# Chunked attention and a one-of-eight expert layer on one core: weights cast by the DMA, records scattered by expert, dense layers in token order

## The chip, the core and the metric

The kernel runs on one core of a Trainium2 chip. Five engines work from queues of their own and meet at semaphores: TensorE (PE; its weight loads are shown as PEld), VectorE (DVE), ScalarE (ACT), GpSimd (POOL) and SyncE (SP), which here only issues transfers. Sixteen DMA engines move the data; SP and POOL each have a queue to them. The metric is the device time of one execution in microseconds, lower is better.

## The reference: what is computed

Inputs are q, k, v (4 batches, 8 heads, 768 positions, 64 wide), eight memory keys and values per head, a gate and eleven weight matrices' worth of layers (two dense, eight experts of two).

```
for each chunk c of 32 positions:                  # attention
    k_full = [mem_k (8), k[c_start-16 : c_end+8]]   # v_full likewise
    a = softmax(q_c @ k_full.T / 8)
    out_c = a @ v_full
x = out as [3072 tokens, 512]                      # the expert layer
y_dense = relu(x @ w1_dense) @ w2_dense
e = argmax(x @ w_gate);  gate = softmax(x @ w_gate)[e]
y = y_dense + gate * (relu(x @ w1[e]) @ w2[e])
```

All weight matrices are 512x512 and lie in DRAM as f32: 18 of them, 1 MB each.

## The kernel before

**Attention.** The work goes in 16 pairs of heads (four pairs make one batch of 768 tokens, six tiles of 128). Each turn of the loop at L478 mixes two or three pairs: POOL casts q and k of pair i+1 to bf16 (`cast_qk`, L234), DVE scales pair i-1 (`scaled`), PE transposes q and k of i+1 (L249), turns back the probabilities of i (L306), transposes x of i-1 for the gate in f32 (`gate_part`, L356), makes scores (L268, L282), gate sums (L371) and values (L318). `load_qk` and `load_v` bring in pair i+2 on SP; `load_v` writes into one of three buffers `vw` that ACT first fills with the memory rows (L207). The order on every engine is the order in which the code is written.

**Weights.** One weight matrix per turn is loaded as f32 into one of three buffers `tmp` on SP (L91, behind the q, k and v loads of the turn) and cast to bf16 by POOL at the end of the next turn (L464). Thirteen are done so; the last five are cast by ACT after the attention.

**Routing.** When the four pairs of a batch are done, `choose` takes each token's expert and `rank` its place among the tokens of that expert. POOL writes the batch's records (x in bf16 and the gate, 1028 bytes) to `x_rec` in DRAM in token order (L449, one DMA). After the last batch DVE and PE turn the ranks into lists (`lane_p`, `lane_t`, `in_tile`; L523 to L581): for each of 31 slots of 128 tokens which expert it holds, which token rows to fetch and where to put the results.

**Slots.** The second stage (L659) takes 31 slots, each of one expert, padded. A slot's records are fetched by an indirect DMA from POOL four slots ahead (L604); PE transposes them (L613); DVE copies the expert's first layer to a fixed place (L635); PE then computes for the slot's tokens both the dense layers (L644 with `w1d`, L668) and the expert's (L644 with `w_st`, L681); DVE adds the two (L687) and POOL scatters the result rows to `out` (L690).

Of the kernel before, what the change touches and what calls it, by code (L numbers as in the profile page):

```python
# [20 lines left out]
def kernel(  # L21
# [31 lines left out]
    NW = 3  # L53
# [21 lines left out]
    wtmp_pool = ctx.enter_context(tc.tile_pool(name="wtmp", bufs=NW))  # L75
# [30 lines left out]
    lane = iota_f32(128, "lane")  # L106
    slot_no = iota_f32(NS, "slot_no")
    desc = iota_f32(E, "desc", base=E, step=-1)
    pcol = iota_f32(1, "pcol", step=0, cm=1)
    ones = r_pool.tile([128, 128], BF16, name="ones")  # L110
# [10 lines left out]
    onehot = r_pool.tile([128, NT, E], BF16, name="onehot")  # L121
    seen = r_pool.tile([128, E], F32, name="seen")
    nc.vector.memset(seen, 0.0)
    seen_bf = r_pool.tile([128, E], BF16, name="seen_bf")
    hi_f = r_pool.tile([128, NT], F32, name="hi_f")
    lane_p = r_pool.tile([128, NT, 128], BF16, name="lane_p")
    lane_t = r_pool.tile([128, NT, 128], BF16, name="lane_t")
    REC = D_moe // 2 + 1
    x_rec = tc.dram_tile([N_tokens, REC], F32, name="x_rec")


    with (
# [207 lines left out]
        def gate_part(pi):  # L340
# [3 lines left out]
            if hp == 0:  # L344
                lg_b = x_pool.tile([128, T, E], F32, tag="lg")
                rec_b = x_pool.tile([128, T, REC], F32, tag="rec")
                bat[b]["lg"], bat[b]["rec"] = lg_b, rec_b
            lg, rec = bat[b]["lg"], bat[b]["rec"]
            nc.gpsimd.tensor_copy(
                rec.bitcast(BF16)[:, :, hp * 128:(hp + 1) * 128], xb  # L350
            )
            xTs_ = []
            for t0 in (0, T // 2):
# [9 lines left out]
                xTs_.append(xT32)  # L363
            st_[pi]["xT"] = xTs_
# [15 lines left out]
        def choose(b):  # L380
# [11 lines left out]
            oh = onehot[:, b * T:(b + 1) * T, :]  # L392
# [8 lines left out]
            nc.vector.reciprocal(rec[:, :, REC - 1:REC], sm)  # L401
            bat[b]["here"] = here

        def rank(b):

            oh = onehot[:, b * T:(b + 1) * T, :]
            rk_ps = g_ps[:, 64:64 + T * E].rearrange("p (t e) -> p t e", e=E)
            nc.tensor.matmul(rk_ps, upper, oh, start=True, stop=False)
            for t in range(T - 1):
                nc.tensor.matmul(  # L410
                    rk_ps[:, t + 1:, :], ones,
                    oh[:, t:t + 1, :].to_broadcast([128, T - 1 - t, E]),
                    start=False, stop=(b == 0 and t == T - 2),
                )
            if b:
                nc.tensor.matmul(
                    rk_ps, ones, seen_bf[:, None, :].to_broadcast([128, T, E]),
                    start=False, stop=True,
                )
# [3 lines left out]
            nc.vector.reduce_sum(rk, val, axis=AX.X)  # L423
            nc.vector.tensor_tensor(seen, seen, bat[b]["here"][:, :, 0], ALU.add)
            nc.vector.tensor_copy(seen_bf, seen)
            rk_i = r_work.tile([128, T], I32, tag="rk_i")
            nc.vector.tensor_copy(rk_i, rk)
            hl_i = r_work.tile([128, 2, T], I32, tag="hl_i")
            nc.vector.tensor_scalar(hl_i[:, 0], rk_i, 127, None, ALU.bitwise_and)
            nc.vector.tensor_scalar(hl_i[:, 1], rk_i, 7, None, ALU.logical_shift_right)  # L430
            lo = r_work.tile([128, T], F32, tag="lo")
            nc.vector.tensor_copy(lo, hl_i[:, 0])
            nc.vector.tensor_copy(hi_f[:, b * T:(b + 1) * T], hl_i[:, 1])
            bat[b]["lo"] = lo

        def lanes(b):
            lo = bat[b]["lo"]
            for t in range(T):
                n = b * T + t
                nc.vector.tensor_scalar(  # L440
                    lane_p[:, n, :], lane, lo[:, t:t + 1], pcol, ALU.is_equal, ALU.mult
                )
                nc.vector.tensor_scalar(
                    lane_t[:, n, :], lane, lo[:, t:t + 1], float(n + 1),
                    ALU.is_equal, ALU.mult,
                )

        def rows_out(b):
            nc.gpsimd.dma_start(  # L449
                x_rec[b * S:(b + 1) * S, :].rearrange("(t p) c -> p t c", p=128),  # L450
                bat[b]["rec"],
            )

        w_todo = list(range(len(w_list)))
        w_tmp = []
        LATE = 5

        def weight_load():
            i = w_todo.pop(0)
            w_tmp.append((i, load_w(*w_list[i])))  # L460

        def weight_cast(eng):
            i, tmp = w_tmp.pop(0)
            eng(w_list[i][1], tmp)  # L464

        with tc.manual_schedule(engines={PE_, DVE_, ACT_, POOL_, SP_}):
            load_qk(0)
            load_small()
            load_qk(1)
            for i in range(2):  # L470
                mem_rows(i)
                load_v(i)
            mem_keys()
            cast_qk(0)
            transpose_qk(0)
            scores(0)
            softmax(0)
            for i in range(NPAIR):  # L478
                nxt = i + 1 < NPAIR
                b, hp = divmod(i, NP)  # L480
                if nxt:
                    cast_qk(i + 1)
                if i + 2 < NPAIR:
                    load_qk(i + 2)
                if i:
                    scaled(i - 1)
                if nxt:
# [236 lines left out]
```

## Time and profile before

| | before |
|---|---|
| median of 3 runs (lowest to highest) | 356.83 us (353.12 to 362.11) |
| the profiled execution | 355.28 us |
| its span, first to last instruction | 353.6 us |
| attention, to the end of the last values | 0 to 202.0 us |
| lists and first fetch | 202.0 to 226.7 us |
| slots | 226.7 to 345.1 us |
| busy: PE, DVE, ACT, POOL | 262.1, 156.1, 141.8, 145.4 us |

Read it in this order. The page gives busy time per engine and, in 40 slices, where it lies, with the clock that PE was granted and how busy the DMA engines were. The windows view gives the same for chosen stretches, with the bytes per second. The timeline gives single instructions: start, length, engine, line, operation, and in brackets the idle time before it and what ended that. A matmul row's length includes the pipeline, so the distance between starts tells what a block of matmuls takes.

### The profile page before, as it was taken

What the parts mean: (1) busy time and instruction counts of PE and PEld (TensorE: products, weight loads), DVE (VectorE), ACT (ScalarE), POOL (GpSimd) and SP (SyncE); (2) the same over time, 40 slices, a digit from 0 to 9 for tenths busy, and PEclk for the clock granted to TensorE, in tenths of its full rate; (3) what the DMA queues carried; (4) which work ended last, traced back from release to release, by engine and by line L of the source; (5) the groups of instructions that cost most, each with busy time, mean ns of one, the idle gap of its engine ahead of it and who ended that gap; (6) DMA issues with size and microseconds to landing.
All of it is one profiled execution on the core that took longest, in us unless ns stands there. A gap on an engine that the chain in (4) does not pass through costs nothing. (4 is left out here: it accounts for less than half of the span.)

```text
span 353.6 us, 10749 instructions
## 1 busy us (share of the span) xinstructions
PE 262.1 (74%) x4577; PEld 214.5 (61%) x4577; DVE 156.1 (44%) x345; ACT 141.8 (40%) x199; POOL 145.4 (41%) x144
## 2 busy tenths in 40 slices
PE   0438566857766785898478852299999999999990
PEld 0337466756655674787466741277777777777760
DVE  3433234437623545544357346244444445445420
ACT  0634334532422542445233244345445444444450
POOL 5202553255054235532612310526656656556431
PEclk9999756765555655556555655599999999999997
DMA  7899999999999999999999229212322332323300
GB/s 167 124 170 223 197 205 241 241 226 200 241 159 217 248 242 224 228 254 235 181 275 260 60 73 302 78 60 83 121 88 86 107 106 84 119 85 110 89 2 0
DMA packets 65615, 56.64 MB, mean 160 GB/s; under 512 B 46910, under 2 KB 46910, under 8 KB 65568
## 3 DMA queue, kind: packets, MB, share of 16 engines
q1 hardware_dynamic: 60768, 42.43, 57.0%
q0 software_dynamic: 4800, 13.54, 12.6%
q8 instruction: 36, 0.59, 0.8%
q14 instruction: 11, 0.09, 0.1%
HBM read 46.50 MB, written 11.28 MB: 163 GB/s over the span
## 5 line engine op out<-in xcount | busy, mean ns | idle before, releaser
L649 ACT ACTIVATE h_sb<-ph 128x512 bf16<-128x512 f32 x62 | 37.0, 597 | 58.4 <-PE ph L644 58.4
L249 PE MATMUL tp_f<-identity,bf 96*128 96x96 bf16 x256 | 25.6, 279 | 37.8 <-POOL bf L237 37.7
L690 POOL DMA_INDIRECT out_dram<-y,dst_i x31 | 31.5, 1016 | 45.0 <-DVE y L687 45.0
L604 POOL DMA_INDIRECT xg<-x_rec,src_i x31 | 37.9, 1224 | 21.5 <-DVE dst_i L581 12.3
L249 PEld LDWEIGHTS <-bf 96*128 96x128 bf16 x256 | 19.7, 136 | 42.9 <-POOL bf L237 42.6
L464 POOL CAST w_all<-tmp 128x2048 bf16<-128x2048 f32 x11 | 20.8, 1893 | 58.8 <-DMA tmp<-in_moe_w_dram 58.8
L371 PE MATMUL at_ps<-wgate,xT 128*128 128x8 f32 x192 | 36.6, 325 | 0.0
L258 ACT COPY dT<-tp_f 128x768 bf16<-128x768 bf16 x16 | 12.8, 797 | 59.5 <-PE tp_f L249 59.5
L371 PEld LDWEIGHTS at_ps<-wgate,xT 128*128 128x128 f32 x192 | 35.1, 280 | 1.4 <-ACT xT L360 0.8
L644 PEld LDWEIGHTS <-w_st 128*128 128x128 bf16 x496 | 30.4, 98 | 7.3 <-issue 0.3
L687 DVE SCALAR_TENSOR_TENSOR y<-py,xg,yd 128x512 f32<-128x512 f32 x31 | 23.3, 750 | 25.7 <-ACT h_sb L649 18.9
L644 PE MATMUL ph<-xT,w1d 128*128 128x128 bf16 x496 | 33.6, 222 | 0.0
L644 PE MATMUL ph<-xT,w_st 128*128 128x128 bf16 x496 | 32.9, 219 | 0.0
L291 DVE TENSOR_REDUCE mx<-sc 128x12 f32<-128x768 f32 x16 | 15.3, 958 | 37.4 <-PE sc L282 37.4
L668 PE MATMUL pd<-w2d,h_sb 128*128 128x512 bf16 x124 | 31.8, 379 | 0.0
L681 PE MATMUL py<-w_all,h_sb 128*128 x124 | 31.8, 379 | 0.0
L617 DVE COPY xT<-xtp 128x512 bf16<-128x512 bf16 x31 | 13.2, 424 | 40.5 <-PE xtp L613 40.5
L318 PE MATMUL av<-vw,at 64*32 64x65 f32 x1536 | 25.1, 284 | 7.7 <-issue 7.5
L644 PEld LDWEIGHTS <-w1d 128*128 128x128 bf16 x496 | 29.9, 100 | 0.2
L356 PE MATMUL xtt<-identity_f,x_p 128*128 128x128 f32 x96 | 24.3, 423 | 7.5 <-DVE x_p L330 7.4
L260 DVE COPY dT<-tp_f 128x768 bf16<-128x768 bf16 x16 | 15.3, 955 | 33.0 <-PE tp_f L249 33.0
L318 PEld LDWEIGHTS av<-vw,at 64*32 64x32 f32 x1536 | 20.8, 132 | 8.9 <-issue 8.3
(139 smaller groups left out, 394.3 us busy)
## 6 DMA issues: line engine op xcount, KB each, us to landing
tmp<-in_moe_w_dram SPq DMA_DIRECT2D x16, 1024.0 KB
vw<-in_v_dram SPq DMA_DIRECT2D x32, 308.0 KB
x_rec<-rec_b POOLq DMA_DIRECT2D x4, 771.0 KB, 8.1
tmp<-in_moe_w_dense_dram SPq DMA_DIRECT2D x2, 1024.0 KB
vw<-in_v_dram SPq DMA_DIRECT2D x32, 10.0 KB
vw<-in_v_dram SPq DMA_DIRECT2D x32, 12.0 KB
xg<-x_rec,src_i POOLq DMA_INDIRECT x31, 3.2
out_dram<-y,dst_i POOLq DMA_INDIRECT x31, 2.8
```

The lines of the kernel that those rows point to most:

```text
L249: nc.tensor.transpose(tp[:, u * PU:(u + 1) * PU], bf[:, u].rearrange("p h d -> p (h d)"), identity[:PU, :PU],)
L318: nc.tensor.matmul(av[cc * CHUNK:(cc + 1) * CHUNK, hh, t * (D + 1):(t + 1) * (D + 1)], at[p0:p0 + KEYS, t, cc * CHUNK:(cc + 1) * CHUNK], v ...
L356: nc.tensor.transpose(xtt[:, t * 128:(t + 1) * 128], xb[:, t0 + t, :], identity_f32)
L371: nc.tensor.matmul(lg_ps[:, i * T // 2 + t, :], xT32[:, t, :], wgate_sb[:, hp, :], start=True, stop=True,)
L464: eng(w_list[i][1], tmp)
L604: nc.gpsimd.indirect_dma_start(xg, None, x_rec, bass.IndirectOffsetOnAxis(ap=src_i[:, s:s + 1], axis=0))
L644: nc.tensor.matmul(ph[:, f, :], w[:, d, f * 128:(f + 1) * 128], xT[:, d, :], start=(d == 0), stop=(d == DT - 1),)
L649: nc.scalar.activation(h_sb, ph, AF.Relu)
L668: nc.tensor.matmul(pd, h_d[:, f, :], w2d_sb[:, f, :], start=(f == 0), stop=(f == FT - 1))
L681: nc.tensor.matmul(py, h_e[:, f, :], w2_all[:, bass.ds(e, 1), f, :], start=(f == 0), stop=(f == FT - 1),)
L687: nc.vector.scalar_tensor_tensor(y, py, xg[:, REC - 1:REC], yd, op0=ALU.mult, op1=ALU.add)
L690: nc.gpsimd.indirect_dma_start(out, bass.IndirectOffsetOnAxis(ap=dst_i[:, s:s + 1], axis=0), y, None, bounds_check=N_tokens - 1, oob_is_er ...
```

## The change

**Weights.** `load_w` issues a DMA from POOL that reads f32 and writes bf16 straight into place. The buffers `tmp` and the casts are gone. One such DMA is issued per turn after `values`, two in each of the last two turns.

**Dense layers.** They are computed in token order for the 24 tiles of tokens. `gate_part` keeps x transposed in bf16 (`xTb`, cast by POOL). The tiles of batch b-1 are done two per turn in the second to fourth turns of batch b (`dense_1`, `dense_2`), 18 tiles; the last batch's six follow the attention. ACT does the relu, DVE (ACT for the last batch) copies the result into the record, which now holds x in bf16, the gate, the token's number and the dense result: 3080 bytes.

**Records.** Each expert has a region of 25 tiles in `x_rec`. `rank` starts from the region's first row, so it gives the row itself. `row_out` scatters a tile of 128 records by an indirect DMA from POOL. The scatters of all tiles are declared independent. After the last `rank`, SP reads the end of each region and writes 128 rows of filler behind it (eight DMAs).

**Slots.** A slot is now 128 consecutive rows of `x_rec`. SP fetches it whole with one plain DMA at a row read from a list; the first fetch waits for every scatter and filler. The dense layers are gone from the loop; ACT instead of DVE copies the transposed records. The place of each result is worked out by two small POOL operations from the token's number in the record. The results' scatters are declared independent as well.

The diff, cut to its core:

```diff
     def load_w(src_ap, dst):
-        tmp = wtmp_pool.tile([128, DT, F], F32, tag="wtmp")
-        nc.sync.dma_start(tmp, src_ap.rearrange("(t p) m -> p t m", p=128))
-        return tmp
+        nc.gpsimd.dma_start(dst, src_ap.rearrange("(t p) m -> p t m", p=128))
...
+    def scattered(ins, group):
+        tc.declare_no_dep(ins.ins, group=group, reason="rows of tokens are distinct")
+        tc.add_to_no_dep_group(group, ins.ins)
...
+                nc_ = nc.vector if last else nc.gpsimd
+                nc_.tensor_copy(
+                    xTb[:, hp, t0 * 128:(t0 + T // 2) * 128],
...
+        def dense_1(b, t):
+            xTb = bat[b]["xTb"]
+            ph = a_ps2.tile([128, 512], F32, tag="tp")
+            for f in range(FT):
+                for d in range(DT):
+                    nc.tensor.matmul(
+                        ph[:, f * 128:(f + 1) * 128],
+                        w1d_sb[:, d, f * 128:(f + 1) * 128],
+                        xTb[:, d, t * 128:(t + 1) * 128],
...
+            nc.scalar.activation(h_d, ph, AF.Relu)
...
+        def dense_2(b, t):
+            pd = a_ps2.tile([128, 512], F32, tag="tp")
...
+            copy = nc.scalar.copy if b == B - 1 else nc.vector.tensor_copy
+            copy(bat[b]["rec"][:, t, YD:], pd)
+
+        def row_out(b, t):
+            n = b * T + t
+            nc.gpsimd.tensor_copy(
+                bat[b]["rec"].bitcast(I32)[:, t, GW + 1:GW + 2], token_i[:, n]
+            )
+            ins = nc.gpsimd.indirect_dma_start(
+                x_rec, bass.IndirectOffsetOnAxis(ap=row_i[:, n:n + 1], axis=0),
+                bat[b]["rec"][:, t, :], None,
+            )
+            scattered(ins, "rows")
...
+            mine = [2 * hp - 2, 2 * hp - 1] if b and hp else []
+            for t in bat[b - 1].pop("ready", []) if b else []:
+                row_out(b - 1, t)
...
+            for _ in range(1 if i + 2 < NPAIR else 2):
+                load_w(*w_todo.pop(0))
...
+        for e in range(E):
+            _, vals = nc.values_load_multi_w_load_instructions(
+                end_i[0:1, e:e + 1], engines=(SP_,),
...
+            ins = nc.sync.dma_start(
+                x_rec[bass.ds(vals[0], 128), :], bat[b - 1]["rec"][:, 0, :]
+            )
+            scattered(ins, "rows")
...
+        for t in range(T):
+            if t + 1 < T:
+                dense_1(b, t + 1)
+            dense_2(b, t)
+            row_out(b, t)
...
         def fetch(s):
...
-            nc.gpsimd.indirect_dma_start(
-                xg, None, x_rec, bass.IndirectOffsetOnAxis(ap=src_i[:, s:s + 1], axis=0)
-            )
+            ins = nc.sync.dma_start(
+                xg[:, None, :],
+                rows_v[bass.ds(r_sp.pop(s), 1), :, :].rearrange("n p c -> p n c"),
+            )
...
+            dst = m_work.tile([128, 1], I32, tag="dst")
+            nc.gpsimd.tensor_tensor(
+                dst, xg.bitcast(I32)[:, GW + 1:GW + 2], keep_i[:, s:s + 1], ALU.mult
+            )
+            nc.gpsimd.tensor_tensor(dst, dst, far_i[:, s:s + 1], ALU.add)
...
+        for s in range(NS):
+            if s + AHEAD < NS:
+                fetch(s + AHEAD)
+            first_layer(s)
+            if s + 2 < NS:
+                transposed(s + 2)
+                staged(s + 2)
+            if s:
+                second_layer(s - 1)
+        second_layer(NS - 1)
```

How the instructions stand. POOL, two turns of the attention before the change (`bf` is q or k in bf16, `rec_b` the batch's records, `w_all` the experts' weights):

```order
L237 CAST bf<-t__1431 96x1024
L237 CAST bf<-t__1433 96x1024
L349 CAST rec_b<-x_p 128x6x128
L464 CAST w_all<-tmp 128x2048
L237 CAST bf<-t__1617 96x1024
L237 CAST bf<-t__1619 96x1024
L349 CAST rec_b<-x_p 128x6x128
L464 CAST w_all<-tmp 128x2048
```

POOL, one turn of the attention with two tiles of dense work, after the change:

```order
L249 CAST bf<-t__1463 96x1024
L249 CAST bf<-t__1465 96x1024
L477 COPY rec_b<-token_i 128x1
L480 DMA x_rec<-rec_b,row_i 25600x770
L477 COPY rec_b<-token_i 128x1
L480 DMA x_rec<-rec_b,row_i 25600x770
L362 CAST rec_b<-x_p 128x6x128
L380 CAST xTb_b<-xT_1771 128x384
L380 CAST xTb_b<-xT_1778 128x384
L88 DMA w_all<-in_moe_w_dram 128x4x512
```

The weight cast that stood ahead of the next casts of q and k is replaced by a DMA issue; two scatters and two casts of x are new.

SP, from the last filler to the seventh fetch, after the change, with what each waits for (DMAHW and DMASW are transfers of SP's and POOL's queues):

```order
L571 DMA x_rec<-rec_b 128x770 [waits DMAHW4_49]
L647 TENSOR_LOAD rb_i [waits DVE_49]
L661 ISA
L661 DMA xg<-x_rec 128x770 [waits DMAHW0_49,DMASW7_49,DMAHW1_49,DMASW6_49,DMAHW2_49,DMASW5_49,DMAHW3_49,DMASW4_49,DMAHW4_49,DMASW3_49,DMAHW5_49,DMASW2_49,DMAHW6_49,DMASW1_49,DMAHW7_49,DMASW0_49,PE_49]
...
L661 DMA xg<-x_rec 128x770 [waits DMAHW5_49,DVE_49,Pool_49]
```

Before, SP ended with its weight loads and the fetches were POOL's. Now the first fetch waits for all transfers in flight, and from the seventh on a fetch waits for DVE and POOL, which free one of six buffers `xg`.

## Rows read from the trace of the kernel before

**Rows 1.** The page: span, and two groups of part 5 (busy us, mean ns).
```profile
span 353.6 us, 10749 instructions
...
L464 POOL CAST w_all<-tmp 128x2048 bf16<-128x2048 f32 x11 | 20.8, 1893 | 58.8 <-DMA tmp<-in_moe_w_dram 58.8
...
L687 DVE SCALAR_TENSOR_TENSOR y<-py,xg,yd 128x512 f32<-128x512 f32 x31 | 23.3, 750 | 25.7 <-ACT h_sb L649 18.9
```

**Rows 2.** Windows: attention, lists, slots; last columns granted clock, DMA share, GB/s.
```profile
26.00:202.00 176.00, 129.46 (x2884) 114.40 (x2884) 79.46 (x175) 66.86 (x89) 67.34 (x59) 0.59 1.02 217
202.00:226.70 24.70, 7.14 (x75) 5.95 (x76) 12.09 (x52) 10.38 (x8) 4.02 (x5) 0.52 0.52 163
226.70:345.10 118.40, 117.78 (x1364) 87.66 (x1364) 54.06 (x91) 55.21 (x93) 66.07 (x59) 0.98 0.28 88
```

**Rows 3.** PE's timeline (start, length, line): values of the first and the last pair.
```profile
19.64 1.63 PE L318 MATMUL av<-vw,at 64*32 64x65 f32 x96
...
200.80 1.18 PE L318 MATMUL av<-vw,at 64*32 64x65 f32 x96
```

**Rows 4.** Waits in total: us, times, longest.
```profile
POOL w_all L464 <- DMA tmp<-in_moe_w_dram: 58.8, 10, 7.4
```

**Rows 5.** Transfers: KB each, or median us from issue to landing.
```profile
tmp<-in_moe_w_dram SPq DMA_DIRECT2D x16, 1024.0 KB
vw<-in_v_dram SPq DMA_DIRECT2D x32, 308.0 KB
...
xg<-x_rec,src_i POOLq DMA_INDIRECT x31, 3.2
out_dram<-y,dst_i POOLq DMA_INDIRECT x31, 2.8
t__161<-in_q_dram SPq DMA_DIRECT2D x1, 384.0 KB
```

**Rows 6.** Windows inside attention and lists: PE first, last columns as in Rows 2.
```profile
77.00:79.00 2.00, 2.00 (x55) 1.65 (x53) 0.00 (x0) 1.50 (x3) 0.00 (x0) 0.50 1.01 337
74.00:76.00 2.00, 1.67 (x17) 1.46 (x18) 0.00 (x0) 0.80 (x1) 1.86 (x3) 0.50 1.10 139
190.00:200.00 10.00, 9.94 (x191) 8.29 (x190) 3.57 (x6) 3.56 (x6) 2.63 (x3) 0.52 0.42 154
210.00:220.00 10.00, 2.52 (x49) 1.82 (x48) 7.98 (x37) 4.96 (x3) 0.83 (x1) 0.50 0.83 237
```

**Rows 7.** Timeline of one slot: PE's blocks, and a fetch on POOL.
```profile
238.48 1.03 PE L668 MATMUL pd<-w2d,h_sb 128*128 128x512 bf16 x4
239.34 0.39 PE L613 MATMUL xtp<-identity,xg 128*128 128x128 bf16 x4
...
240.46 1.03 PE L681 MATMUL py<-w_all,h_sb 128*128 x4
...
241.32 1.06 PE L644 MATMUL ph<-xT,w_st 128*128 128x128 bf16 x16
242.21 1.03 PE L668 MATMUL pd<-w2d,h_sb 128*128 128x512 bf16 x4
...
251.40 1.44 POOL L604 DMA_INDIRECT xg<-x_rec,src_i  x1 [0.30 <-issue]
```

**Rows 8.** Timeline from the last rank to the first slots.
```profile
210.54 0.16 DVE L427 CAST rk_i<-rk 128x6 int32<-128x6 f32 x1
...
226.36 0.95 POOL L604 DMA_INDIRECT xg<-x_rec,src_i  x1 [0.30 <-issue]
226.69 0.58 PE L613 MATMUL xtp<-identity,xg 128*128 128x128 bf16 x4 [8.75 <-DMA xg<-x_rec,src_i]
...
228.25 1.91 PE L644 MATMUL ph<-xT,w1d 128*128 128x128 bf16 x16
```

**Rows 9.** Timeline of the start: q's first load, and the cast that waits for it.
```profile
1.29 0.49 SPq L199 DMA_DIRECT2D t__161<-in_q_dram  x1
...
5.53 1.03 POOL L237 CAST bf<-t__161 96x1024 bf16<-96x1024 f32 x1 [2.00 <-DMA t__161<-in_q_dram]
```

More of the change, by code (lines that the diff above doesn't have):

```diff
@@ L351, in gate_part @@
             )
+            last = pi == NPAIR - 1
             xTs_ = []
@@ L412, in rank @@
                     oh[:, t:t + 1, :].to_broadcast([128, T - 1 - t, E]),
-                    start=False, stop=(b == 0 and t == T - 2),
+                    start=False, stop=False,
                 )
[L415 to L418, printed above, removed]
-                )
+            nc.tensor.matmul(
+                rk_ps, ones, seen_bf[:, None, :].to_broadcast([128, T, E]),
+                start=False, stop=True,
+            )
             val = r_work.tile([128, T, E], F32, tag="val")
@@ new lines @@
+        w_todo = list(w_list)
+        load_qk(0)
+        load_small()
+        load_qk(1)
+        for i in range(2):
+            mem_rows(i)
+            load_v(i)
+        mem_keys()
+        cast_qk(0)
+        transpose_qk(0)
+        scores(0)
+        softmax(0)
+        for i in range(NPAIR):
+            nxt = i + 1 < NPAIR
+            b, hp = divmod(i, NP)
+            if nxt:
+                cast_qk(i + 1)
+            mine = [2 * hp - 2, 2 * hp - 1] if b and hp else []
+            for t in bat[b - 1].pop("ready", []) if b else []:
+                row_out(b - 1, t)
+            if i + 2 < NPAIR:
+                mem_rows(i + 2)
+                load_qk(i + 2)
+                load_v(i + 2)
+            if i:
+                scaled(i - 1)
+            if nxt:
+                transpose_qk(i + 1)
+            probs_back(i)
+            for t in mine[:1]:
+                dense_1(b - 1, t)
+            if i:
+                gate_part(i - 1)
+            if nxt:
+                scores(i + 1)
+                softmax(i + 1)
+            for t in mine[:1]:
+                dense_2(b - 1, t)
+            for t in mine[1:]:
+                dense_1(b - 1, t)
+            if i:
+                gate_sum(i - 1)
+            values(i)
+            for t in mine[1:]:
+                dense_2(b - 1, t)
+            if mine:
+                bat[b - 1]["ready"] = mine
+            for _ in range(1 if i + 2 < NPAIR else 2):
+                load_w(*w_todo.pop(0))
+            if hp == 0 and b:
+                choose(b - 1)
+            if hp == 1 and b:
+                rank(b - 1)
+            if hp == NP - 1 and b:
+                for t in bat[b - 1].pop("ready"):
+                    row_out(b - 1, t)
@@ new lines @@
+        b = B - 1
+        scaled(NPAIR - 1)
+        gate_part(NPAIR - 1)
+        gate_sum(NPAIR - 1)
+        dense_1(b, 0)
+        choose(b)
+        rank(b)
+        cnt_ps = g_ps[:, 112:112 + E]
+        nc.tensor.matmul(cnt_ps, ones, seen_bf, start=True, stop=True)
+        cnt = r_work.tile([128, E + 1], F32, tag="cnt")
+        nc.vector.memset(cnt[:, E:], 0.0)
+        nc.vector.scalar_tensor_tensor(
+            cnt[:, :E], region, -128.0, cnt_ps, op0=ALU.mult, op1=ALU.add
+        )
@@ L616, in transposed @@
             xT = m_work.tile([128, DT, 128], BF16, tag="xT")
[L617 removed]
+            nc.scalar.copy(xT, xtp)
             xTs[s] = xT
[L620 to L628 removed]
         def staged(s):
             if s % GRP == 0:
[L633 removed]
+                listed(DVE_, et_i, s, e_dve, E - 1)
             w_st = m_work.tile([128, DT, F], BF16, tag="w_st")
```

324 lines of the change are left out of this document (121 added, 203 removed).

## The prediction

> **What bounds the kernel now.** I read the page, then the windows by stage, the chain of waits, and the timeline of one pair, of the lists and of one slot. The sum is made against the profiled execution, 355.3 us, whose span is 353.6 [rows 1]; the 1.7 us around it are added back at the end. The median of the runs is 0.4% above it. Three stages stand out [rows 2].
>
> In the attention the values of the first pair end at 21.3 us and those of the last at 202.0 [rows 3]: 12.05 us a pair. The DMA share there is 1.02 and PE is busy 74% of the time. What moves per pair is 1.05 MB of weight, 0.79 MB of q and k, and 0.66 MB of v (two loads of 308 KB and small ones) [rows 5]. The windows give two rates [rows 6]: 337 GB/s where the long pieces pass, 139 where v's pieces of 256 bytes do. 1.84 MB at 337 take 5.4 us and v at 139 takes 4.7: a floor of **10.1 us a pair**. The rest is a knot: POOL's weight cast waits 5.9 us a turn for its load [rows 4], and the casts of q and k that PE needs stand behind it.
>
> In the slots PE is the bound: 117.8 of 118.4 us busy at a clock of 0.98 [rows 2], and a slot lasts from 238.48 to 242.21, 3.73 us [rows 7]. Between them lie the lists, 24.7 us [rows 2].
>
> **The change part by part.**
>
> *Weights.* Thirteen POOL casts of 1.89 us [rows 1] and the wait ahead of them go; five casts on ACT at the end go too. All 18 MB are still read. No row shows a casting DMA, so I bound it: at the rate of long pieces counted by bytes written, 0.52 MB, it takes 1.6 us; by bytes read 3.1; at v's 139 GB/s 7.5. I take 3.1, since the pieces in DRAM are the same 2 KB as now. So the floor of 10.1 stays. A pair without dense work then needs PE 8.9 us (129.5 of 176 us at a mean clock of 0.59 [rows 2]) and DMA 10.1; I take **10.8** instead of 12.05, the floor and some of today's gap. There are six such pairs after the first.
>
> *Dense layers in the attention.* Nine pairs get two tiles. A tile is 16 matmuls of 128 columns and 4 of 512: 1.75 us by one slot's blocks at full clock [rows 7], about 3.5 at the low one (there the 16 alone take 1.91 with the pipeline [rows 8]). PE's work in such a pair is then some 16.1 us with the low clock throughout (a little over 8.9, and 7.0), and some 11 at full. DMA gets two scatters of 394 KB, 2.3 us at 337 GB/s: 12.4. So a pair lasts between 12.4 and 16.1; I take **14.0**, the middle, since PE is granted 0.59 on average now [rows 2] and dense blocks raise it for a part of the pair. It also holds the two places where the next casts of q and k stand behind scatters that wait for the turn's last dense tile. [...]
>
> POOL, DVE and ACT are busy 38 to 45% of the attention now [rows 2]; POOL trades the weight cast for two casts of x, two scatters and an issue of about 1 us each, ACT and DVE get two tiles' relus and copies: at most 3 us more a pair on each, beside PE's work. The last values end at 21.3 + 6 x 10.8 + 9 x 14.0 = **212.1**.
>
> *Lists.* Today the last rank is out at 210.5, 8.5 us after the last values, and the first transposes start at 226.7 [rows 8]. That rank stays. Then PE has eleven half tiles, 9.6 us at full clock, 19 at the low one; I take 11.5 (the first two blocks low). Add 2 us for the last copy and scatter. On the DMA side six scatters and eight fillers, 5.5 MB, take 16 us at 337 GB/s or 19 at 285 (237 GB/s at a share of 0.83 [rows 6]). So all rows have landed 25 to 28 us after the last values, and a fetch adds some 3 [rows 5]: **30** in place of 24.7. With the low clock it is 35; with everything best, 25. DVE's lists for whole tiles lie behind the dense work, and the weights' last two loads, 6 us, land before the fillers.
>
> *Slots.* The loop loses a 16-matmul block and a 4-matmul block. What stays is 239.34 to 240.46 (transposes and one first layer) and 240.46 to 241.32 (second layer), 1.98 us [rows 7]. Two other things come near. The fetch: buffer six means that the fetch for four slots ahead waits for DVE's sum of two slots back, which ends about 1.05 us into the slot (0.75 us [rows 1] after the last second layer, and the way between engines), and its tile is wanted 0.9 us into the slot after next. With L from issue to use the period is (L + 0.15)/2 if that is over 1.98. The nearest rows for L are 3.2 us for a third of the bytes [rows 5] and 4.2 for a load of 384 KB on SP [rows 9]: 1.98 to 2.2. And the bytes: 394 KB in and 262 KB out, 656 KB, take 1.95 us at 337 GB/s and 2.3 at 285. I take **2.25 a slot**, near the upper ends since both load the same engines; 31 slots are 69.8 in place of 31 x 3.73 = 115.6. DVE and ACT, busy 54.1 and 55.2 us in 31 slots now [rows 2], 1.75 and 1.78 each, have less to do than that. POOL has one issue of 0.95, 0.3 behind it [rows 8], and two operations on one number per partition; between nothing and 0.3 each, 1.3 to 1.9.
>
> *Ends.* From the first transposes to the first layer 1.6 us [rows 8]; the last second layer 1.1; from PE's end to the span's end 8.5, as now (345.1 to 353.6).
>
> Sum: 212.1 + 30 + 1.6 + 69.8 + 1.1 + 8.5 = 323.1, and 1.7 around it: **325 us**, 9% below the median.
>
> **The rivals.**
>
> *All best.* The clock goes up in the dense pairs and the slots run at PE's rate: 21.3 + 6 x 10.1 + 9 x 12.4 = 193.5; lists 25; slots 61.4; with the ends 291, **293 us**. For it: the slots, bf16 blocks of full size alone, have 0.98 [rows 2]. Against it: the 190 to 200 row. Chance 14%. [...]
>
> *The clock stays low.* Dense pairs 16.1, lists 35: the last values at 231, the sum 347, **349 us**. For it: the attention's mean is 0.59, and 0.52 where PE was busiest [rows 2, 6]. Against it: the slots, which begin after 0.52, have a mean of 0.98 [rows 2]. Chance 13%.
>
> *The slots find a new wait.* L of 5.2 us, or POOL: its issue takes 1.44 beside DVE's copy against 0.95 without [rows 7, 8], and with small operations held up as well it comes to 2.7 a slot: 14 us more, **339 us**. [...] If the scatters should wait for each other after all, six of 1.0 + 2.8 us replace the 13.5 of the last batch, some 10 more, **335**. Together 13%.
>
> *The casting DMA is slow.* One mechanism on the other side: at the 139 GB/s of short pieces a weight takes 7.5 us instead of 3.1, 4.4 more in each pair, on a queue that is full already. Pairs last 14.5 and 16.8, the last values end at 259.5, the sum is 370.5, **372 us**. It decides from 3.9 us more per weight (7.0 each, 150 GB/s read). For it: nothing in the trace casts, and long pieces do not prove the rate. Against it: the pieces are eight times v's. Chance 10%.
>
> **The numbers.** The forecast's own case, 305 to 338, has 50%. What a measurement of this kernel can tell from no change is about 2%, 349.7 to 364.0 us here. Faster: 50 + 14 + 13, and half of the low-clock case: 83%. Within 2%: the other half, 7%. Slower: 10%. The range from 294 to 352 holds the forecast, the new wait, about two thirds of the low clock and more than half of the best case: 80%.
>
> **What would show it.** Values of the last pair end near 212; pairs alternate between about 11 and 14 us, and POOL no longer waits for weights. The first transposes come 30 us after the last values, with the fetch waiting for the last rows. Slots start every 2.25 us, PE waiting at the transposes for the fetch. It is wrong if a weight takes much over 3 us of DMA time, if the clock in the dense pairs is near 0.5 or near 1.0 throughout, or if the slots go at 1.98 or over 2.6.

## The result and the profile after

The changed kernel takes **324.36 us** (median of 4 runs, 322.27 to 329.71) beside 357.44 for the kernel before (4 runs, 353.12 to 362.11). The ratio is **0.909**, 95% interval 0.897 to 0.921: 9% faster, where 325 us had been forecast. The execution that was profiled is the longest of the four, 329.7 us with a span of 328.0, so its rows add up to 5 us more than the median. Medians here are of all runs of a kernel and ratios of its faster runs alone; where those are too few, no ratio is given.

The windows of its three stages answer to [rows 2]: pairs from the end of the first values to the end of the last, lists up to the first transposes, and slots up to 0.7 us past the end of TensorE's work (319.2). The columns are the same.

```profile
23.10:208.30 185.20, 140.47 (x3242) 116.63 (x3243) 79.11 (x146) 76.76 (x107) 88.41 (x125) 0.85 1.10 191
208.30:244.00 35.70, 19.73 (x151) 14.46 (x151) 12.91 (x48) 8.19 (x15) 9.57 (x14) 0.68 0.77 219
244.00:319.90 75.90, 66.29 (x744) 48.35 (x744) 39.89 (x58) 34.59 (x62) 45.79 (x86) 0.97 0.75 238
```

Beside [rows 2], the attention is 6 us longer though nine pairs carry two dense tiles more, and the granted clock in it is 0.85 in place of 0.59. The lists are 11 us longer. The slots are 42 us shorter, but now TensorE is busy for only 66 of their 76 us, and DMA's share is 0.75 in place of 0.28.

The terms of the forecast stand beside what the trace has. Two further traces of the same kernel, of the runs below, follow in brackets.

| us | forecast | measured |
|---|---|---|
| last values end | 212.1 | 208.3 (211.0, 208.3) |
| from there to the first transposes | 30 | 35.7 (33.9, 34.1) |
| first transposes to first layer | 1.6 | 2.1 |
| 31 slots | 69.8 | 72.1, 2.33 each |
| last second layer | 1.1 | 1.0 |
| TensorE's end to the span's end | 8.5 | 8.8 |
| span | 323.1 | 328.0 |

Two rows of the page carry what is new. The first is the group of the sixteen casting weight loads into `w_all`, with KB written and median us to landing; the second is the page's row of DMA queues for them (packets, MB, share).

```profile
w_all<-in_moe_w_dram POOLq DMA_DIRECT2D x16, 512.0 KB, 8.7
...
q0 software_dynamic: 13904, 25.20, 33.9%
```

A casting load is 8.7 us on its way, longer than any price in the forecast. That is its latency among other transfers, not what it costs: the experiments price it.

The waits in total name what replaced [rows 4]. POOL's wait for weights is gone; these are the places where a slot now waits, and the one where SP does in the attention (us, times, longest).

```profile
SPq L230 <- ACT vw L219: 48.2, 12, 8.3
SPq L661 <- DVE y L728: 43.9, 24, 7.5
...
PE xtp L679 <- DMA xg<-x_rec: 19.8, 12, 12.0
...
DVE y L728 <- DMA out_dram<-y,dst: 9.6, 7, 2.3
```

Read from the bottom: in 7 slots DVE's sum waits for an earlier result to be scattered, SP's next fetch waits for DVE's sum, and TensorE waits for the fetch (of the 19.8 us, 12.0 are the first fetch). The chain of a slot thus leads to the scatter of results, which POOL issues.

### The profile page after: what moved, and what is told of

It reads as the page before. It is cut to its first block, busy times and chain, and to the rows that moved or that the text cites. A ratio compares the mean times of both kernels' runs of the same rounds, so it can differ in the third digit from the quotient of the medians.

```text
span 328.0 us, 10539 instructions
## 1 busy us (share of the span) xinstructions
PE 234.6 (72%) x4390; PEld 186.1 (57%) x4390; DVE 141.6 (43%) x278; ACT 128.8 (39%) x193; POOL 155.6 (47%) x255
## 3 DMA queue, kind: packets, MB, share of 16 engines
q0 software_dynamic: 13904, 25.20, 33.9%
## 4 chain that ended last, share of the span: by engine, by line
PE 39%; DMA 25%; DVE 9%; issue 8%; SPq 7%; POOL 6%; ACT 4%; POOLq 0%; ACTq 0%; DVEq 0%
DMA xg<-x_rec 10%; PE at_ps L392 5%; DMA vw<-in_v_dram 5%; PE pd L468 5%; PE ph L454 5%; PE xtt L370 4%; PE av L330 4%; PE py L716 4%; SPq L238 3%; PE ph L701 3%; PE at_ps L318 3%; DMA t__2883<-in_q_dram 2%; POOL out_dram L731 2%; DMA x_rec<-rec_b 2%; DMA x_rec<-rec_b,row_i 2%
## 5 line engine op out<-in xcount | busy, mean ns | idle before, releaser
L480 POOL DMA_INDIRECT x_rec<-rec_b,row_i x24 | 24.5, 1020 | 54.4 <-issue 20.1
L731 POOL DMA_INDIRECT out_dram<-y,dst x31 | 32.2, 1039 | 28.3 <-DVE w_st L691 16.8
L728 DVE SCALAR_TENSOR_TENSOR y<-py,xg 128x512 f32<-128x512 f32 x31 | 23.3, 751 | 31.4 <-PE py L716 21.7
L454 PEld LDWEIGHTS <-w1d 128*128 128x128 bf16 x384 | 28.1, 111 | 10.6 <-issue 8.1
L701 PE MATMUL ph<-xT,w_st 128*128 128x128 bf16 x496 | 33.9, 223 | 0.0
L261 PE MATMUL tp_f<-identity,bf 96*128 96x96 bf16 x256 | 20.8, 246 | 17.9 <-POOL bf L249 16.6
L454 PE MATMUL ph<-xTb_b,w1d 128*128 128x128 bf16 x384 | 30.2, 242 | 4.3 <-ACT dT L270 4.3
L219 ACT COPY vw<-mv_all 128x1536 f32<-128x1536 f32 x16 | 23.5, 1472 | 24.3 <-PE av L330 16.5
L706 ACT ACTIVATE h_sb<-ph 128x512 bf16<-128x512 f32 x31 | 18.5, 597 | 33.0 <-PE ph L701 33.0
L691 DVE COPY w_st<-w_all 128x2048 bf16 x31 | 21.3, 694 | 21.4 <-PE ph L701 18.6
L380 POOL CAST xTb_b<-xT 128x384 bf16<-128x384 f32 x30 | 14.9, 507 | 29.8 <-ACT xT L374 29.4
L330 PEld LDWEIGHTS av<-vw,at 64*32 64x32 f32 x1536 | 18.8, 115 | 17.5 <-issue 15.5
L468 PE MATMUL pd<-w2d,h_d 128*128 128x512 bf16 x96 | 28.3, 424 | 0.3 <-ACT xT L374 0.3
L310 ACT ACTIVATE a_sb<-dif 128x768 f32<-128x768 f32 x16 | 13.5, 843 | 37.8 <-DVE dif L305 37.8
L679 PE MATMUL xtp<-identity,xg 128*128 128x128 bf16 x124 | 12.8, 229 | 19.8 <-DMA xg<-x_rec 19.8
## 6 DMA issues: line engine op xcount, KB each, us to landing
w2d<-in_moe_w_dense_dram POOLq DMA_DIRECT2D x1, 512.0 KB, 12.5
```

The source lines that it names most:

```text
L219: nc.scalar.copy(vw[pi % NV][:, :, :D], mv_all[:, pi:pi + 1, :].to_broadcast([128, NCH, D]),)
L261: nc.tensor.transpose(tp[:, u * PU:(u + 1) * PU], bf[:, u].rearrange("p h d -> p (h d)"), identity[:PU, :PU],)
L330: nc.tensor.matmul(av[cc * CHUNK:(cc + 1) * CHUNK, hh, t * (D + 1):(t + 1) * (D + 1)], at[p0:p0 + KEYS, t, cc * CHUNK:(cc + 1) * CHUNK], v ...
L454: nc.tensor.matmul(ph[:, f * 128:(f + 1) * 128], w1d_sb[:, d, f * 128:(f + 1) * 128], xTb[:, d, t * 128:(t + 1) * 128], start=(d == 0), st ...
L468: nc.tensor.matmul(pd, h_d[:, f * 128:(f + 1) * 128], w2d_sb[:, f, :], start=(f == 0), stop=(f == FT - 1),)
L480: ins = nc.gpsimd.indirect_dma_start(x_rec, bass.IndirectOffsetOnAxis(ap=row_i[:, n:n + 1], axis=0), bat[b]["rec"][:, t, :], None,)
```

## The experiments

All are compared with runs of the kernel before on their own chip (medians 355.3 to 357.0 us).

**The changed kernel again**, twice.

> The changed kernel once more, for a second trace of it beside the others. It should take 322 to 330 us, with the last values of the attention at 204 to 210 us, some 35 us from there to the first transposes of the slots and 2.2 to 2.4 us a slot. If the first pairs again take longer than before the change although POOL waits for no weight, that is the kernel and not that one execution.

> The changed kernel itself once more, beside the three that follow on the same chip: 322 to 330 by both theories.

Measured: 329.21 us in one run; in the later set 326.14 (4 runs, 319.42 to 330.02). So differences under some 5 us between versions of this kernel are not told apart by their medians; the stages in their traces repeat better, each to some 3 us, and are used below.

**The casting loads alone, in the kernel before.**

```
-        tmp = wtmp_pool.tile([128, DT, F], F32, tag="wtmp")
-        nc.sync.dma_start(tmp, src_ap.rearrange("(t p) m -> p t m", p=128))
-        return tmp
+        nc.gpsimd.dma_start(dst, src_ap.rearrange("(t p) m -> p t m", p=128))
...
-                    weight_cast(nc.gpsimd.tensor_copy)
+                for _ in range(1 if i + 2 < NPAIR else 2):
+                    load_w(*w_list[w_todo.pop(0)])
```

> The kernel before with the casting DMA alone, issued from POOL at the end of a turn where its weight cast stood; records, lists and slots as before. Theory of the prediction (a casting load takes the DMA engines the 3.1 us of a plain one, and POOL's wait goes): pairs of about 10.8 us, last values near 183 in place of 202, and the casts after the attention gone: 330 to 338 us. Rival (a casting load costs the engines clearly more than a plain one, as the first pairs of the changed kernel suggest with 13.6 us): pairs of 13 or more, last values at 215 or later, 360 to 372 us, slower than before. In between, 345 to 357: both hold in part and cancel.

Measured: 341.06 us, ratio 0.961 (0.956 to 0.966). The time lies a little above the 330 to 338 that the forecast's theory had. The last values end at 187.4 instead of 202.0. The window of its fifteen pairs:

```profile
23.80:187.40 163.60, 122.30 (x2884) 107.72 (x2884) 78.39 (x177) 66.40 (x89) 55.53 (x63) 0.69 1.09 193
```

163.6 us are 10.9 a pair, where 10.8 had been forecast for a pair without dense work. So the weight path alone brings 14 us of the whole change's 33, and the slow casting DMA is refuted. The DMA share rises to 1.09, POOL's work falls to 55.5 us, and its wait for weights is gone.

**Six loads more, casting or plain.** Two kernels add six loads of 1 MB in the turns 1 to 3, to places that later loads overwrite.

```
+            for j in range(2) if 1 <= i <= 3 else ():
+                src = moe_w2[2 * i + j - 2].rearrange("(t p) m -> p t m", p=128)
+                nc.gpsimd.dma_start(w_list[-1 - 2 * (i - 1) - j][1], src)
```

The plain one loads the same megabytes as f32, as two DMAs of half a matrix each:

```
+                for h in range(2):
+                    place = w_list[-1 - 4 * (i - 1) - 2 * j - h][1]
+                    nc.gpsimd.dma_start(
+                        place.bitcast(F32).rearrange("p (a b) m -> p a (b m)", b=2),
+                        src[:, 2 * h:2 * h + 2, :],
+                    )
```

> The changed kernel with six more casting weight loads (1 MB read, 0.5 MB written each), two in each of the turns 1 to 3, into places that later loads overwrite. If a casting load costs by the bytes that it reads, 3.1 us each, and the DMA engines are what the first pairs wait for: 19 us more, 343. If it costs by the bytes that it writes, 1.6 us each: 9 us more, 334. If it goes at the rate of short pieces, 7.5 us each: 45 us more, 369. If the first pairs wait for something else than the DMA engines: within 4 us of 324.

> The changed kernel with the same six MB more, read from the same matrices in the same turns, but loaded as f32 without a cast (twice the bytes written). If the cast costs nothing beside the read, this takes as long as with the six casting loads, within 3 us; if the DMA engines are what the first pairs wait for, 19 us more than the changed kernel, 343. If the cast slows the engines, it is faster than the six casting loads, by 26 us where these take 7.5 us each.

Measured: 341.23 us with the casting loads, ratio 0.946 (0.938 to 0.954), and 347.32 with the plain ones, 0.974 (0.968 to 0.981). Over the changed kernel's 324.4 and 326.1 that is 15 to 17 us, and 21 to 23; by the ends of the last values, below, it is 13 and 22. That makes **2.2 to 2.8 us a casting load, 3.5 to 3.8 a plain one**. A casting load is thus priced between its bytes written (1.6) and its bytes read (3.1), and far from 7.5. The traces show when it is paid. The last part of the fifth pair's values in the changed kernel (the second trace in the table above), then the fifth pair's values with six casting loads, and with six plain ones (start, length):

```profile
73.93 1.09 PE L330 MATMUL av<-vw,at 64*32 64x65 f32 x52 [1.75 <-issue]
```
```profile
79.43 1.18 PE L330 MATMUL av<-vw,at 64*32 64x65 f32 x96
```
```profile
88.83 1.17 PE L330 MATMUL av<-vw,at 64*32 64x65 f32 x96
```

They end at 75.0, 80.6 and 90.0, 6 and 15 us apart from the first (five traces of the changed attention have 70.3 to 77.5); the last values end at 221.9 and 230.5, where the five have 204.0 to 211.4, 208.6 on average: 13 and 22 us. What the fifth pair waits for is a load of q, in flight beside the added ones. This is POOL's cast of it, with the casting loads and with the plain ones:

```profile
70.60 1.04 POOL L249 CAST bf<-t__821 96x1024 bf16<-96x1024 f32 x1 [14.26 <-DMA t__821<-in_q_dram]
```
```profile
81.32 1.03 POOL L249 CAST bf<-t__825 96x1024 bf16<-96x1024 f32 x1 [17.27 <-DMA t__825<-in_q_dram]
```

The longest waits for such a cast, and for TensorE behind it, are 15.1 and 19.8 us on TensorE, 16.6 and 20.3 on DVE, 14.3 and 18.8 on ACT: for some ten microseconds ahead of it no engine computes. So transfers in the first turns are on the path of the attention, a cast on the way adds nothing that these runs show, and the casting load is the cheaper one. That the f32 load costs more because it writes twice the bytes is likely but not shown alone: it is also issued as two DMAs of 0.71 us on POOL for one of 0.75, 4 us more in the three turns.

**No dense tiles in the attention.** The dense layers of the first three batches are left out (their part of the record is zero); the scatters stay.

```
         def dense_1(b, t):
+            if b < B - 1:
+                return
...
         def dense_2(b, t):
+            if b < B - 1:
+                nc.vector.memset(bat[b]["rec"][:, t, YD:], 0.0)
+                return
```

> The changed kernel without the dense layers of the first three batches (18 of 24 tiles): their part of the result is zero. Theory of the prediction (PE sets the pairs with dense work, at 14 us against 10.8): nine pairs lose 2 to 3 us each, the last values come 18 to 28 us earlier. Rival (those pairs are set by the transfers and the copies around them, and PE's dense blocks stand where it would wait): 0 to 6 us earlier. A third outcome, no gain and a lower clock: the dense blocks had held the clock up for the f32 work.

Measured: 309.4 us, ratio 0.868 (0.863 to 0.873). The window of its pairs:

```profile
24.30:190.20 165.90, 120.77 (x2886) 107.00 (x2885) 77.03 (x147) 66.39 (x89) 86.34 (x122) 0.67 1.16 207
```

That is 11.1 us a pair, close to the 10.9 of the kernel before with casting loads: the scatters and the casts of x cost the attention next to nothing. The eighteen dense tiles cost 15 to 17 us by the medians and 19 by the windows (185.2 against 165.9; 23 and 19 with the two further traces), not the 29 of the forecast (nine pairs by 3.2). The rows say why. TensorE's busy time differs by 19.7 us (140.5 against 120.8), although eighteen tiles at full clock are 18 x 1.75 = 31.5. The granted clock is 0.85 with them (0.81 and 0.82 in the further traces) and 0.67 without: the other work of the pairs got faster. The gate sums, for one, which the edit does not touch, take a mean of 301 ns without the tiles and 276 with them:

```profile
L392 PE MATMUL at_ps<-wgate,xT 128*128 128x8 f32 x192 | 32.2, 301 | 0.0
```
```profile
L392 PE MATMUL at_ps<-wgate,xT 128*128 128x8 f32 x192 | 27.4, 276 | 0.0
```

**The loads of v freed from ScalarE.**

```
-            nc.scalar.copy(
-                vw[pi % NV][:, :, :D],
-                mv_all[:, pi:pi + 1, :].to_broadcast([128, NCH, D]),
-            )
+            rows = [(0, 128)] if pi < NV else [(0, n_mem), (KEYS, KEYS + n_mem)]
+            for r0, r1 in rows:
+                nc.scalar.copy(
+                    vw[pi % NV][r0:r1, :, :D],
+                    mv_all[r0:r1, pi:pi + 1, :].to_broadcast([r1 - r0, NCH, D]),
+                )
```

> The changed kernel, but from the fourth pair on ScalarE writes only the sixteen rows of the memory values (two copies of 8 partitions instead of one of 128), so that the loads of v on SP's queue no longer wait for ScalarE. If that wait (SP 48.2 us for ScalarE, TensorE 14 us for v's loads) holds up the pairs: 8 to 14 us less, 310 to 316. If the DMA engines are the limit of the attention: within 4 us of 324, with the wait moved to the loads themselves.

Measured: 329.85 us, ratio 0.924 (0.916 to 0.932): no gain. The waits of SP in this kernel:

```profile
SPq L232 <- PE av L332: 29.5, 5, 8.4
...
SPq L232 <- ACT vw L221: 5.9, 2, 4.9
SPq L232 <- DMA vw<-in_v_dram: 5.4, 12, 0.9
```

SP's 48.2 us for ScalarE became 29.5 for TensorE's values, which free the buffer, and the pairs did not get shorter (last values at 212.2). A long wait on a queue that runs ahead of its consumer was no bound.

**Sixteen fillers in place of eight.**

```
+        end2_i = r_pool.tile([128, E], I32, name="end2_i")
+        nc.vector.tensor_scalar(end2_i, cnt_ps, 128.0, None, ALU.add)
+        for e in range(E):
...
+            ins = nc.sync.dma_start(
+                x_rec[bass.ds(vals[0], 128), :], bat[b - 1]["rec"][:, 0, :]
+            )
```

> The changed kernel with sixteen fillers instead of eight behind the last rank (the further eight one tile behind the first, 394 KB each). If the fetch of the first slot waits because the DMA engines are full of scatters and fillers: 3.15 MB more at 285 to 337 GB/s, 9 to 11 us more, 334. If it waits for TensorE's dense tiles and the last scatter behind them, with room beside it: 0 to 3 us more, 325 to 327.

Measured: 338.0 us, ratio 0.937 (0.927 to 0.948), 10 to 14 us over the changed kernel. Its windows of the lists and its first transposes:

```profile
220.00:230.00 10.00, 8.12 (x73) 5.96 (x73) 6.65 (x34) 3.95 (x8) 2.14 (x3) 0.69 0.63 202
230.00:240.00 10.00, 4.06 (x36) 2.14 (x33) 1.86 (x3) 3.06 (x6) 5.34 (x9) 0.83 1.00 341
240.00:250.00 10.00, 0.00 (x0) 0.00 (x0) 0.00 (x0) 0.00 (x0) 0.00 (x0) 0.50 0.93 326
```
```profile
254.59 0.61 PE L692 MATMUL xtp<-identity,xg 128*128 128x128 bf16 x4 [20.54 <-DMA xg<-x_rec]
```

From the last values (211.4) to these transposes it is 43.1 us, 9 more than the 33.9 and 34.1 of the changed kernel's two later traces: 3.15 MB at 340 GB/s. For ten microseconds no engine computes at all while the DMA engines are full. SP issues a filler only every 1.1 us, so its last one goes out late, at 240.4; but it then takes 10.9 us to land, at a DMA share of 1.00 and 0.93 (start, length in the chain of waits):

```profile
240.37 10.90 DMA x_rec<-rec_b
```

The end of the lists waits for bytes.

**Deeper buffers in the slots**: nine record buffers for six, fetches six slots ahead for four, six result buffers for three.

```
-        tc.tile_pool(name="m_load", bufs=6) as m_load,
+        tc.tile_pool(name="m_load", bufs=9) as m_load,
+        tc.tile_pool(name="m_out", bufs=6) as m_out,
...
-        AHEAD = 4
+        AHEAD = 6
...
-            y = m_work.tile([128, D_moe], F32, tag="y")
+            y = m_out.tile([128, D_moe], F32, tag="y")
```

> The changed kernel with nine buffers for fetched tiles in place of six, fetched six slots ahead in place of four, and six buffers for results in place of three. Theory (the slot is held by a ring of waits: the fetch waits for the sum of two slots back, and that for a result buffer whose scatter has not landed): a slot falls from 2.3 to PE's 2.0 us, the kernel gains 8 to 11 us, near 315. Rival (the DMA engines are full: 656 KB a slot at the 271 GB/s of the stretch are 2.4 us): no gain, within 2 us.

Measured: 322.43 us, ratio 0.903 (0.896 to 0.911), not told apart from the changed kernel. Yet the timeline of TensorE in its slots shows the first layers at their floor:

```profile
256.73 1.06 PE L702 MATMUL ph<-xT,w_st 128*128 128x128 bf16 x16
257.62 0.39 PE L680 MATMUL xtp<-identity,xg 128*128 128x128 bf16 x4
...
258.70 1.06 PE L702 MATMUL ph<-xT,w_st 128*128 128x128 bf16 x16
...
260.69 1.06 PE L702 MATMUL ph<-xT,w_st 128*128 128x128 bf16 x16
```

1.98 us a slot, the very period worked out from [rows 7] (2.09 over all slots). So the waits for buffers did hold TensorE. The gain is given back behind it: TensorE ends 15.5 us before the span does, against 8.8. POOL's timeline at the end of the same kernel, when TensorE and the fetches are done (in brackets the idle time before and what ended it):

```profile
310.75 0.99 POOL L732 DMA_INDIRECT out_dram<-y,dst  x1 [0.60 <-POOL dst L727]
311.76 0.22 POOL L724 TENSOR_TENSOR dst<-xg,keep_i 128x1 int32<-128x1 int32 x1
312.05 0.19 POOL L727 TENSOR_TENSOR dst<-dst,far_i 128x1 int32<-128x1 int32 x1
312.84 0.99 POOL L732 DMA_INDIRECT out_dram<-y,dst  x1 [0.60 <-POOL dst L727]
```

The last sum on DVE starts at 307.42, the last scatter at 317.0. POOL still goes through its scatters one after the other, **2.09 us each**: 0.99 to issue, two operations of 0.2, and 0.60 in which the issue waits for the second of them. In mid-slots, beside DVE's copies, the same chain of the changed kernel reads:

```profile
273.36 0.99 POOL L731 DMA_INDIRECT out_dram<-y,dst  x1 [0.28 <-POOL dst L726]
274.37 0.21 POOL L723 TENSOR_TENSOR dst<-xg,keep_i 128x1 int32<-128x1 int32 x1
274.66 0.19 POOL L726 TENSOR_TENSOR dst<-dst,far_i 128x1 int32<-128x1 int32 x1
275.90 0.99 POOL L731 DMA_INDIRECT out_dram<-y,dst  x1 [1.05 <-DVE w_st L691]
276.91 0.23 POOL L723 TENSOR_TENSOR dst<-xg,keep_i 128x1 int32<-128x1 int32 x1
277.21 0.53 POOL L726 TENSOR_TENSOR dst<-dst,far_i 128x1 int32<-128x1 int32 x1
278.01 0.99 POOL L731 DMA_INDIRECT out_dram<-y,dst  x1 [0.28 <-POOL dst L726]
```

2.54 and 2.11 us, some 2.33 on average. Two things lie beside them on DVE: the sum that the scatter at 275.90 sends, and the copy of an expert's layer next to the small operation that takes 0.53:

```profile
274.37 0.75 DVE L728 SCALAR_TENSOR_TENSOR y<-py,xg 128x512 f32<-128x512 f32 x1 [1.34 <-DMA out_dram<-y,dst]
...
277.01 0.68 DVE L691 COPY w_st<-w_all 128x2048 bf16 x1
```

All 16 POOL instructions that are lengthened in these slots (a small operation over 0.4 us, an issue over 1.15) lie beside such a copy. The step of 2.54, though, is one whose scatter follows its own sum closely, 0.78 us behind its end. In this execution 18 of the 31 scatters start within 1.1 us of the end of their sum, so POOL is not the only limit in it. In the two further traces only 5 and 4 do, and with deep buffers one does: there the scatters fall behind, by up to 10 us. What a fetch waits for says the same, since POOL's small operations read a tile before its buffer is free (this execution, the second further trace, deep buffers):

```profile
SPq L661 <- POOL dst L726: 7.8, 7, 1.9
```
```profile
SPq L661 <- POOL dst L726: 26.2, 21, 1.9
```
```profile
SPq L662 <- POOL dst L727: 32.3, 18, 2.6
```

**A smaller record**: the dense result is kept in bf16, 2056 bytes a record for 3080.

```
-    REC = YD + D_moe
+    REC = YD + D_moe // 2
...
-            copy(bat[b]["rec"][:, t, YD:], pd)
+            copy(bat[b]["rec"].bitcast(BF16)[:, t, 2 * YD:], pd)
...
-                y, py, xg[:, GW:GW + 1], xg[:, YD:], op0=ALU.mult, op1=ALU.add
+                y, py, xg[:, GW:GW + 1], xg.bitcast(BF16)[:, 2 * YD:], op0=ALU.mult, op1=ALU.add
```

> The changed kernel with the dense result kept in bf16 in the record: 2056 bytes instead of 3080, so 131 KB less in every scatter, filler and fetch. If the DMA engines' bytes are what the attention, the lists and the slots wait for: the attention loses 18 x 131 KB (7 to 8 us at 285 to 337 GB/s), the lists 14 x 131 KB (5.5 us at 330), the slots 31 x 0.1 to 0.25 us: 14 to 20 us less, 305 to 311. If only the lists wait for bytes: 318. If TensorE and the engines' waits set all three: 322 to 326.

> The same with nine record buffers in place of six, fetches six slots ahead and six result buffers. If a slot waits for buffers to come free (the fetch for DVE's sum two slots back, DVE for the scatter of a result): down to TensorE's 2.0 us a slot, 5 to 9 us less than with the smaller record alone. If a slot waits for bytes: within 2 us of it.

Measured: 321.92 us, ratio 0.904 (0.897 to 0.911), with the smaller record; 315.89 (4 runs, 307.42 to 319.32) with the deep slots as well. By stages, the lists take 31.0 and 29.0 us, 3 to 5 less than 34, most of what 1.83 MB at 340 GB/s are (5.4). The attention is no shorter (last values at 213.4 and 207.4): the 2.4 MB that its scatters save come in later turns, and there they were hidden, as the loads of the first turns are not. So of the forecast 14 to 20 us only the lists' part came. In the slots the period stays. The windows of 50 us of slots, with the large and the small record:

```profile
255.00:305.00 50.00, 43.37 (x500) 31.34 (x498) 28.69 (x42) 23.22 (x42) 33.12 (x64) 1.00 0.85 264
```
```profile
255.00:305.00 50.00, 45.81 (x530) 33.85 (x536) 30.92 (x46) 24.61 (x46) 32.60 (x66) 1.00 0.67 222
```

DMA's share falls from 0.85 to 0.67, TensorE gets ahead by a little, and POOL does the same. From first to last scatter the 31 results take, in lines of the changed kernel, of deep slots, of the small record, and of both (ns min/median/max, first and last start):

```profile
L731 POOL DMA_INDIRECT out_dram<-y,dst x31: 992/995/1447, 252.3 to 324.4; - x31
```
```profile
L732 POOL DMA_INDIRECT out_dram<-y,dst x31: 992/995/1507, 246.8 to 317.0; - x31
```
```profile
L731 POOL DMA_INDIRECT out_dram<-y,dst x31: 992/994/1421, 251.9 to 321.3; - x31
```
```profile
L732 POOL DMA_INDIRECT out_dram<-y,dst x31: 995/1000/1499, 244.3 to 313.6; - x31
```

72.1, 70.2, 69.4 and 69.3 us for thirty steps: 2.40, 2.34, 2.31 and 2.31 (2.35 and 2.36 in the further traces of the changed kernel). Neither buffers nor bytes move it by more than 0.1.

**Four buffers of v**, in the kernel with both, filled with the memory values a turn earlier.

```
-        NV = 3
+        NV = 4
...
-                mem_rows(i + 2)
                 load_qk(i + 2)
                 load_v(i + 2)
+            if i + 3 < NPAIR:
+                mem_rows(i + 3)
```

> The kernel with the smaller record and the deep slots, and four buffers of v in place of three, filled with the memory values a turn earlier. If the loads of v wait for a buffer (SP 41 to 48 us for ScalarE or TensorE) and that holds up the pairs: 8 to 14 us less than the kernel without it. If the DMA engines are the limit of the attention: within 3 us of it.

Measured: 325.92 us, ratio 0.909 (0.902 to 0.917); last values at 215.2. No gain, so the loads of v wait for nothing that a buffer gives. Of the 10 us over the kernel without it, 7.8 lie before the last values; why stays open.

The version that came out fastest is the small record with deep slots, 315.9 us, 3% under the changed kernel of the same set by their medians, but with spreads of 12 and 11 us. What follows the last values repeats better: 116.5 to 119.7 us in the three traces of the changed kernel, 116.5 with deep slots, 111.4 with the small record, 109.8 with both. It is the record that shortens this part. Of the 7.6 us between the traces of the last two, 6.0 lie in the attention, where both are the same kernel.

## Why the prediction was right, and where it wasn't

The forecast's own case held: faster by 9%, by the parts that it named. Point by point:

- **Casting loads, 3.1 us by bytes read: near, a little too much.** Added ones cost 2.2 to 2.8. The rival of the slow casting DMA is refuted by the casting loads alone in the kernel before, which gained 4%.
- **A pair without dense work, 10.8: right in two kernels without any (10.9 and 11.1), wrong for those pairs of the changed kernel.** There the first four pairs and two more took 17.4, 15.8, 7.9, 13.4, 12.0 and 13.0 us, 13.2 on average (12.8 and 13.0 in the further traces). The first four after the start take 46 to 54 us in every kernel without added loads, the one before with its 48.5 included: the forecast took an even pace where there is none, and the added loads show that transfers count there. The two later ones are not without dense work: the second layer of a turn's second tile stands behind `values`, so the next pair has it. Without the dense tiles these two take 8.8 and 9.0; whether that block explains the whole difference is not settled.
- **A pair with two dense tiles, 14.0: too long.** The nine took 11.8 us on average (12.5 and 11.9 in the further traces). That is no proof against the DMA floor of 12.4, since the last of them have few loads beside them, and without the last three it is 12.3 to 13.8. The step that failed is "the middle, since PE is granted 0.59 on average now": the dense blocks raised the granted clock of the whole attention from 0.67 to 0.85, and the 31.5 us of tiles added 19.7 to TensorE's busy time. A smaller part of the rise, from 0.59 to 0.69, came with the casting loads alone. The row of 0.52 that I held against a higher clock (190 to 200 us in [rows 6]) has no dense block in it, only f32 blocks, transposes of 128 columns among them, and two short bf16 ones. The same ten microseconds of the changed kernel, with dense blocks among them, have 1.00:

```profile
190.00:200.00 10.00, 8.95 (x234) 7.41 (x231) 5.92 (x13) 4.38 (x7) 6.95 (x11) 1.00 0.48 112
```

- These two errors cancel, by luck: 6 x 2.4 too little and 9 x 2.2 too much. With first values that end 1.8 us later than before, the last values came 3.8 us early.
- **Lists, 30: too short by 4 to 6.** The mechanism was right, and the fillers show it: what is added in bytes comes out at 340 GB/s. The size was off in three places. The rank came 10.6 us after the last values for 8.5, since DVE copied a dense result ahead of the last batch's x. TensorE's dense tiles ran at the low clock until some 225 (granted 0.51 from 219.4 to 225.0, and 1.00 from there to 232.1) and ended at 232.0, so the last scatter was issued at 233.9, 25.6 us after the values. And it was 7 us on its way among the other scatters and fillers, so that all rows had landed 32.4 us after the values, for 25 to 28. So in the changed kernel both count, the late last scatter and the bytes queued before it. The chain of waits has this last piece (start, length):

```profile
233.93 6.82 DMA x_rec<-rec_b,row_i
```

- **Slots, 2.25: nearly right, for another reason.** Measured are 2.31 to 2.40. The step that failed is "near the upper ends since both load the same engines": with less to move the period stayed, and with deeper buffers TensorE ran at 1.98 while results piled up. What sets it is POOL, which the forecast put at 1.3 to 1.9 a slot. Its chain is 2.09 us undisturbed, with 0.60 between the second small operation and the issue where the forecast had 0.3; and DVE's copies, beside which an issue of 0.99 takes up to 1.45 and a small operation of 0.2 up to 0.75, bring it to some 2.3. The third rival had POOL as the bound at 2.7; it came, at a price of 2 to 5 us in the whole and not 14. The forecast's own wait, the fetch behind the sum of two slots back, was real too. In the profiled execution 19 of 25 fetches go out within 0.2 us of that sum and their tiles are used 4.5 us later (median), which by its (L + 0.15)/2 is some 2.3: in that execution the two limits are about equally long. In the two further traces L is 4.0 and 3.8, which gives 2.1 and 2.0, and the period of 2.32 is POOL's. That taking the two small operations out of POOL's chain would bring the slots to 2.0 is argued from these rows; it was not tried.
- **Ends** were right (8.8 for 8.5), but only while TensorE is held back together with POOL: with deep slots this end is 15.5 us.

The clock that stays low is refuted (0.81 to 0.85 in three traces); the case of all best had the clock's rise right and lost its 30 us to the first pairs, the lists and POOL.

## What to carry to other kernels

The slots, once they had lost their bound, were set by the next serial chain: add such a chain up with the waits between its instructions. Here three short operations on POOL made 2.09 us, 0.60 of them a wait. A second execution of the same kernel can have another limit in front, so read more than one trace before naming it. When deeper buffers bring an engine to its floor and the time stays, look at what drains behind its end. And a forecast by sums can be right by errors that cancel: only kernels that take out one term (no dense tiles, casting loads alone) showed which terms were.

## What the runs showed of the hardware

- A casting DMA of a 1 MB matrix cost 2.2 to 2.8 us in the whole time where plain loads of the same bytes read, as two DMAs each, cost 3.5 to 3.8; the issue of one into `w_all` took POOL 0.74 to 0.81 us, against 0.99 for a scatter of results.
- Between the small POOL operation that makes an address and the scatter that uses it lie 0.60 us in each of the last five slots of the changed kernel, behind DVE's last copy. Where that operation itself took 0.52 to 0.67 us beside DVE's copy and the issue waited for it, 0.28 to 0.30 followed.
- Beside DVE's bf16 copy of an expert's layer, and in the slots only there, POOL's issues took up to 1.45 us for 0.99 and its small operations 0.52 to 0.75 for 0.18 to 0.25. The small operations, which issue no transfer, are held up like the issues; why, no row shows.
- More matrix work made the attention's other matrix work faster: granted clock 0.67 without the dense tiles, 0.81 to 0.85 with them, and 301 against 276 ns for a matmul of the gate sums.
